# Decode attention beside a gated feed-forward block: all loads behind w_up's go through GpSimd's software queue

## The chip, the core and the metric

The kernel runs on one core of a Trainium2 chip. A core has TensorE (PE, matrix products), VectorE (DVE), ScalarE (ACT), GpSimd (POOL) and SyncE (SP), each with an instruction queue of its own, and 16 DMA engines that move data between the chip's memory (HBM) and the core's on-chip memory (SBUF). Engines wait for each other by semaphores. A transfer is issued by an instruction in the queue of SyncE, ScalarE or GpSimd; on the first two hardware makes the list of row transfers from the instruction, on GpSimd software does. The metric is the device time of one execution, in microseconds (us); the time of a kernel is the median of several runs.

## The reference

Four sequences (B = 4), one new token each (512 numbers). Attention has 32 heads of 128 numbers over a cache of 4096 keys and values per head, all in 32-bit floats:

```python
q = (x @ wq).reshape(B, 1, 32, 128).transpose(0, 2, 1, 3)
p = softmax(einsum("bhqd,bhkd->bhqk", q, k_cache) * 128 ** -0.5)
a = einsum("bhqk,bhkd->bhqd", p, v_cache).transpose(0, 2, 1, 3).reshape(B, 1, 4096) @ wo
b = (gelu(x @ w_gate) * (x @ w_up)) @ w_down
g = sigmoid((x * gate_w).sum(-1, keepdims=True))
out = g * a + (1 - g) * b
```

The inner size of the feed-forward block is 1792. The two caches are 268 MB each and are read once; the weights are some 28 MB together.

## The kernel before

**Tiles.** The attention is cut into NT = 32 tiles, each of one sequence and four heads. Tile i has one load of keys, K(i), and one of values, V(i), of 128 rows of 64 KiB each (8 MiB). K(i) lies 32 partitions per head and 128 keys per partition. For a tile DVE multiplies the keys by the query (`products`, L384), sums over the 128 numbers of each key (`sums`, L390), and finds the greatest score (`soft_max`, L395 to L397); ACT makes the exponentials (L402); PE multiplies them with the values (`pv`, L416). `products` and `sums` are each done in two parts, a quarter of 4096 numbers per partition (`shared` is True) and the rest of 12288.

**One buffer for everything.** All loads go into one SBUF tensor, `big`. The two places for keys overlap by a quarter, the part called shared: K(i+1) may be loaded as soon as the shared quarter of K(i) is summed. There is one place for values: V(i) may be loaded when `pv(i - 1)` is through. Before the tiles the same space holds wq, w_gate and w_up; behind them w_down and wo.

**The order.** `Plan` takes the steps in the order of the program text (`add`), and works out for each step which earlier steps it must wait for, by the ranges that they read and write. `loop` turns the repeated tiles on PE, DVE and ACT into loops; SyncE's and GpSimd's steps are written out one by one. An engine works through its own queue in order. Every load is made by `load` (L258), so all 76 of them stand in SyncE's queue in the order: wq, K(0), w_gate, w_up, K(1), V(0), K(2), V(1), ..., V(31), w_down, and wo in eight pieces. ACT issues the two small loads x and gate_w (L292, L293). GpSimd has six small instructions at the start and one at the end.

**The start.** wq lands, PE forms the queries (L330), DVE and PE spread them (L347 to L374). w_gate and w_up may be loaded when PE has read wq. K(1) waits for `sums(0, True)`. In between, with i = 0, stands the feed-forward block's first half:

```python
        products(i, False)
        if i == 0:
            gates()
            ffn_up(0)
            ffn_up(1)
            ffn_gelu()
            load_kv("v", 0)
        sums(i, False)
```

`ffn_up(0)` and `ffn_up(1)` are PE's products with w_gate and w_up (L518). `ffn_gelu` works in w_up's place (L530 to L537), so it begins when PE has read w_up. V(0) takes space that the block's intermediate numbers lie in, so it waits for its last step, the transposition into `hT` (L537). K(2) waits for `sums(1, True)`, which stands behind all that on DVE.

**The end.** `load_d` and `load_w` load w_down and wo; PE multiplies with them (L497, L505), and SyncE stores the result in two parts (L616).

Of the kernel before, what the change touches and what calls it, by code (L numbers as in the profile page):

```python
# [19 lines left out]
class Plan:  # L20
# [18 lines left out]
    def add(self, engine, emit, reads=(), writes=(), lane=None, unit=1):  # L39
        lane = lane or engine  # L40
        self.units[lane] = unit
        row = self.by_lane.setdefault(lane, [])
        step = Step(lane, engine, emit, self.turn if engine in self.loops else None)
        step.at = len(row)
        need = {}
        for accesses, writing in ((reads, False), (writes, True)):
            for name, lo, hi in accesses:
                for other, a, b, wrote in self.past.get(name, ()):
                    if a < hi and lo < b and (wrote or writing):
                        if other.lane == engine and engine == "pe":  # L50
                            continue
                        if other.lane == engine and not wrote:
                            continue
                        need[other.lane] = max(need.get(other.lane, -1), other.at)
        seen = self.seen[engine]
        for l, n in sorted(need.items(), key=lambda x: -len(self.by_lane[x[0]])):
            if seen.get(l, -1) >= n:
                continue
            other = self.by_lane[l][n]
            other.asked = True  # L60
            step.waits[l] = n
            seen[l] = n
            for k, v in self.knew[other].items():
                seen[k] = max(seen.get(k, -1), v)
        step.waits = {l: n for l, n in step.waits.items()
                      if not any(self.knew[self.by_lane[m][k]].get(l, -1) >= n for m, k in step.waits.items() if m != l)}
        self.knew[step] = dict(seen)
        self.knew[step][lane] = step.at
        if row and lane == engine:
            for k, v in self.knew[row[-1]].items():  # L70
                if k != lane:
                    self.knew[step][k] = max(self.knew[step].get(k, -1), v)
        for accesses, writing in ((reads, False), (writes, True)):
            for name, lo, hi in accesses:
                old = self.past.get(name, [])
                if writing:
                    old = [x for x in old if not (lo <= x[1] and x[2] <= hi)]
                self.past[name] = old + [(step, lo, hi, writing)]
        row.append(step)
        self.steps.append(step)  # L80
        return step
# [51 lines left out]
def tile_gated_mix(tc: tile.TileContext, x, kc, vc, wq, wo, w_gate, w_up, w_down, gate_w, out):  # L133
    nc = tc.nc
# [107 lines left out]
    plan = Plan(nc)  # L242
    add = plan.add
    V, A, T, G = nc.vector, nc.scalar, nc.tensor, nc.gpsimd
# [11 lines left out]
        return g if plan.k is None else plan.k  # L256

    def load(dst, src, writes, lane):  # L258
        return add("sp", lambda: nc.sync.dma_start(dst, src), (), writes, lane=lane, unit=16)

    def load_kv(kind, i):
        src = (vc, kc)[kind == "k"]
        a = KB_ * (i % 2) if kind == "k" else VA if i < NT - 1 else 0
        s = src[i % B, HT * (i // B):HT * (i // B) + HT].rearrange("h (p r) d -> (h p) (r d)", p=PH)
        load(place(a, TW), s, [z(a, TW)], "vl" if kind == "v" and i == NT - 1 else kind)
# [7 lines left out]
    def load_f(s):  # L273
        load(place((F0, F1)[s], KC * F), (w_gate, w_up)[s].rearrange("(p c) n -> p (c n)", c=KC),
             [z((F0, F1)[s], KC * F)], f"f{s}")

    def load_d():
        load(place(D0, FC * DM), w_down.rearrange("(p i) n -> p (i n)", i=FC), [z(D0, FC * DM)], "k")
# [326 lines left out]
    for h in range(2):  # L605
# [4 lines left out]
        for c, move in ((2 * h + 1, act), (2 * h, dve)):  # L610
            dst, read, write = res[:B, slice(*COLS[c])], [(("acc", "po0")[h], 0, C4)], [("res", *COLS[c])]
# [48 lines left out]
```

## Time and profile before

| | |
|---|---|
| median of 3 runs | 1308.88 us (1308.85 to 1308.92) |
| the profiled execution | 1308.95 us, its span 1307.5 us |
| DVE busy | 1158.2 us (89% of the span) |
| PE busy | 353.2 us (27%) |
| ACT busy | 87.3 us (7%) |
| POOL busy | 0.7 us, 6 instructions |
| moved by DMA | 564.83 MB, 432 GB/s over the span |

The profile names instructions by engine, line of the kernel and tiles (`big<-in_A_k_cache` is a load of keys). The span runs from the first to the last instruction; the execution's own time is 1.45 us longer. An idle time is given with what ended it. The DMA view of a stretch shows how busy the 16 engines were in 40 equal slices, and for each queue the packets (one row of a load, or the 4 bytes that raise a semaphore), their bytes and the share of the 16 engines' time that they took; a packet counts where it starts, so a short window can show over 100%. q1 is SyncE's queue and q10 is ACT's.

### The profile page before, as it was taken

How to read it: one execution, taken by the hardware profiler on the slowest of the kernel's cores; microseconds unless marked ns; L12 is line 12 of the kernel's file. 1: busy time of each engine (PE TensorE's matmuls, PEld its weight loads, DVE VectorE, ACT ScalarE, POOL GpSimd, SP SyncE). 2: the span in 40 equal slices, each digit the busy share in tenths (PEclk: the TensorE clock that was granted, in tenths of full speed). 3: DMA queues.
4: the chain of work that ended last, by engine and by line, in shares of the span. 5: the costliest groups of instructions: out<-in, count | busy, mean ns of one | idle time of the engine just before them, and what ended most of it. 6: DMA issues, size and time to landing. Idle time of an engine off the chain costs nothing.

```text
span 1307.5 us, 6158 instructions
## 1 busy us (share of the span) xinstructions
PE 353.2 (27%) x2512; PEld 100.2 (8%) x2512; DVE 1158.2 (89%) x303; ACT 87.3 (7%) x291; POOL 0.7 (0%) x6
## 2 busy tenths in 40 slices
PE   2303233212232211322321222321133232123227
PEld 0100001000010000100000000100001000000003
DVE  2799999999899998989989898998989899898992
ACT  0000000000000000000000000000000000000001
POOL 0000000000000000000000000000000000000000
PEclk9656666556666656666655666665666665666668
DMA  9999999999999999999999999999999999999998
GB/s 418 424 439 439 430 441 428 439 427 441 425 441 425 441 427 439 435 433 439 431 439 429 439 427 441 425 441 425 441 433 433 439 431 439 431 439 428 439 428 370
DMA packets 10986, 564.83 MB, mean 432 GB/s; under 512 B 1232, under 2 KB 1752, under 8 KB 1888
## 3 DMA queue, kind: packets, MB, share of 16 engines
q1 hardware_dynamic: 10960, 564.67, 99.8%
q8 instruction: 7, 0.11, 0.0%
q14 instruction: 3, 0.02, 0.0%
q10 hardware_dynamic: 16, 0.02, 0.0%
HBM read 564.67 MB, written 0.01 MB: 432 GB/s over the span
## 4 chain that ended last, share of the span: by engine, by line
DMA 72%; DVE 26%; PE 1%; issue 1%; ACT 0%; SPq 0%; DVEq 0%
DMA big<-in_A_k_cache 66%; DVE sc L390 13%; DVE big L384 12%; DMA big<-in_B_w_up 2%; DMA big<-in_A_wo 2%; DMA big<-in_A_wq 2%; PE po L330 1%; PE q L518 0%; PE acc L505 0%; PE wide L497 0%; PE po L505 0%; DVE hT L537 0%; DVE big L535 0%; DVE big L530 0%; DVE big L534 0%
## 5 line engine op out<-in xcount | busy, mean ns | idle before, releaser
L384 DVE TENSOR_TENSOR big<-big,qb 128x4096 f32<-128x4096 f32 x64 | 556.0, 8687 | 89.5 <-DMA big<-in_A_k_cache 89.5
L390 DVE TENSOR_REDUCE sc<-big 128x32 f32<-128x4096 f32 x64 | 555.9, 8686 | 2.3
L416 PE MATMUL po<-big,PM 128*32 128x512 f32 x2048 | 295.9, 743 | 899.9 <-DMA big<-in_A_v_cache 899.9
L416 PEld LDWEIGHTS po<-big,PM 128*32 128x32 f32 x2048 | 72.7, 133 | 1116.7 <-DMA big<-in_A_v_cache 823.9
L402 ACT ACTIVATE PM<-sc,nb 32x128 f32<-32x128 f32 x128 | 67.2, 525 | 476.4 <-DVE nb L397 430.7
L424 ACT ACTIVATE o<-po 128x512 f32<-128x512 f32 x16 | 9.6, 597 | 446.2 <-PE po L416 446.2
L402 ACT ACTIVATION_READ_ACCUMULATOR PM<-sc,nb 32x1 f32 x128 | 26.1, 204 | 0.0
L374 ACT ACTIVATE qb<-q 128x512 f32<-128x512 f32 x8 | 4.8, 597 | 245.7 <-PE q L372 245.7
L347 DVE TENSOR_TENSOR big<-po,amask 128x512 f32<-128x512 f32 x2 | 1.3, 686 | 18.0 <-PE po L330 18.0
L433 PE MATMUL sm<-o,sel 128*16 128x128 f32 x128 | 15.4, 273 | 5.8 <-ACT o L424 5.8
L518 PE MATMUL q<-big,xT 128*32 128x448 f32 x64 | 9.5, 751 | 18.0 <-DMA big<-in_B_w_gate 13.0
L330 PE MATMUL po<-big,xT 128*32 128x512 f32 x64 | 8.7, 702 | 18.9 <-DMA big<-in_A_wq 18.9
L433 PEld LDWEIGHTS sm<-o,sel 128*16 128x16 f32 x128 | 11.7, 97 | 14.4 <-ACT o L424 13.1
L615 DVE COPY res<-acc 4x144 f32<-4x144 f32 x1 | 0.3, 296 | 12.7 <-PE acc L505 12.7
L372 PE MATMUL q<-QM,hc 128*128 128x512 f32 x16 | 9.3, 666 | 4.2 <-DVE hc L368 4.2
L395 DVE TENSOR_REDUCE m<-sc 128x1 f32<-128x128 f32 x32 | 9.2, 286 | 1.1
L440 DVE RECIPROCAL ri<-sm 16x1 f32<-16x1 f32 x8 | 1.2, 156 | 8.7 <-PE sm L435 8.7
L396 DVE STREAM_TRANSPOSE mt<-m 128x32 f32<-128x32 f32 x32 | 6.8, 212 | 1.1
L397 DVE TENSOR_REDUCE nb<-mt 128x1 f32<-128x32 f32 x32 | 5.9, 186 | 1.1
L497 PE MATMUL wide<-big 128*32 128x512 f32 x46 | 5.6, 596 | 1.9 <-DMA big<-in_A_wo 1.9
L320 DVE TENSOR_TENSOR big<-big 4x512 f32<-4x512 f32 x1 | 0.7, 679 | 4.8 <-DMA big<-in_gate_w 4.8
L518 PEld LDWEIGHTS q<-big,xT 128*32 128x32 f32 x64 | 2.9, 146 | 23.8 <-issue 23.8
(74 smaller groups left out, 59.8 us busy)
## 6 DMA issues: line engine op xcount, KB each, us to landing
big<-in_A_wo SPq DMA_DIRECT2D x1, 4096.0 KB, 28.3
big<-in_B_w_gate SPq DMA_DIRECT2D x1, 3584.0 KB, 18.9
big<-in_B_w_up SPq DMA_DIRECT2D x1, 3584.0 KB, 28.1
big<-in_B_w_down SPq DMA_DIRECT2D x1, 3584.0 KB, 19.0
big<-in_A_wo SPq DMA_DIRECT2D x1, 1792.0 KB, 26.4
big<-in_A_wo SPq DMA_DIRECT2D x1, 1280.0 KB, 29.1
big<-in_A_k_cache SPq DMA_DIRECT2D x32, 29.7
big<-in_A_v_cache SPq DMA_DIRECT2D x32, 29.3
```

Of the source, the lines that this page charges most:

```text
L330: last = T.matmul(PO[s][32 * j:32 * j + 32].rearrange("p j d -> p (j d)"), xTf[:, c, :32], w[:, n0:n0 + HB * D], start=c == 0, stop=c == K ...
L372: pe(lambda: T.matmul(q.rearrange("p b d -> p (b d)"), HC.rearrange("p h k -> p (h k)"), QM.rearrange("p b d -> p (b d)"), start=True, sto ...
L384: dve(lambda: V.tensor_tensor(k, k, QB[:, b:b + 1, :].to_broadcast([P, r1 - r0, D]), op=OP.mult), m + t("qb"), m)
L390: dve(lambda: V.tensor_reduce(SC[i % 2][:, r0:r1], k, axis=AX.X, op=OP.add), [z(KA(i) + r0 * D, (r1 - r0) * D)], [(f"sc{i % 2}", r0, r1)])
L395: dve(lambda: V.tensor_reduce(M1[n], SC[n], axis=AX.X, op=OP.max), t(f"sc{n}"), t(f"m1{n}"))
L396: dve(lambda: V.transpose(MT, M1[n].to_broadcast([P, PH])), t(f"m1{n}"), t("mt"))
L397: dve(lambda: V.tensor_reduce(NB[n], MT, axis=AX.X, op=OP.max, negate=True), t("mt"), t(f"nb{n}"))
L402: last = A.activation(PM[:, PZ:].rearrange("p (c m) -> p c m", m=32)[s, :, h:RJ * HT:HT], SC[n][s, :].rearrange("p (c j) -> p c j", j=RJ), ...
L416: last = T.matmul(PO[n][32 * c:32 * c + 32].rearrange("p j d -> p (j d)"), PM[:, m0:m0 + 32], place(VAT(i) + j * N, N), start=b == 0 and j ...
L424: act(lambda: A.activation(O[n], PO[n], AF.Copy), t(f"po{n}"), t(f"o{n}"))
L433: T.matmul(sm[:B * HT, :D], selv[:, j, m0:m0 + B * HT], O[n][:, j, :], start=(n, j) == (0, 0), stop=(n, j) == (N - 1, RJ - 1))
L518: last = T.matmul(q.rearrange("p b d -> p (b d)")[32 * j:32 * j + 32, :FG], xTf[:, c, :32], place((F0, F1)[s] + c * F + j * FG, FG), start ...
```

## The change

`load` counts the steps that SyncE has. The first four loads (wq, K(0), w_gate, w_up) stay with it, all later ones are issued by GpSimd, whose transfers have a queue of their own; their semaphores get new names. Nothing else differs: the same 76 loads of the same shapes, into the same places, behind the same waits.

```diff
     def load(dst, src, writes, lane):
-        return add("sp", lambda: nc.sync.dma_start(dst, src), (), writes, lane=lane, unit=16)
+        e, queue = ("sp", nc.sync) if sum(x.engine == "sp" for x in plan.steps) < 4 else ("pool", G)
+        return add(e, lambda: queue.dma_start(dst, src), (), writes, lane=lane if e == "sp" else "p" + lane, unit=16)
```

One line more in the code makes every line number behind L259 greater by one. SyncE's queue at the start, before (a row names the line, the operation, the tile and its source, the shape, and the queues whose semaphores it waits for: `lane_dve` is DVE's progress, `lane_pe` PE's):

```order
L259 DMA big<-in_A_k_cache 128x16384
L627 UNCONDITIONAL_BRANCH
L259 DMA big<-in_B_w_gate 128x7168 [waits barrier_Pool_Activation_PE_DVE_SP_release,lane_pe]
L259 DMA big<-in_B_w_up 128x7168
L259 DMA big<-in_A_k_cache 128x16384 [waits lane_dve]
L259 DMA big<-in_A_v_cache 128x16384 [waits lane_dve]
L259 DMA big<-in_A_k_cache 128x16384 [waits lane_dve]
```

The rows are K(0), w_gate, w_up, K(1), V(0) and K(2): K(1) stands behind w_up in one queue. SyncE's queue from the same place, now:

```order
L260 DMA big<-in_A_k_cache 128x16384
L628 UNCONDITIONAL_BRANCH
L260 DMA big<-in_B_w_gate 128x7168 [waits barrier_Pool_Activation_PE_DVE_SP_release,lane_pe]
L260 DMA big<-in_B_w_up 128x7168
L617 DMA out<-res 4x288 [waits lane_fin0]
L617 DMA out<-res 4x224 [waits lane_fin1]
```

Behind w_up only the two stores are left. GpSimd's queue, before, from its own instructions for the identity matrix to its end:

```order
L298 MEMSET ident 128x128 [waits barrier_Pool_Activation_PE_DVE_SP_gather]
L299 ISA [waits lane_pool]
L299 AFFINE_SELECT ident<-ident 128x128
L635 ISA [waits issued]
L635 ISA
```

Between the identity matrix and the clearing of the semaphores at the end there was nothing. GpSimd's queue now, from the same place:

```order
L299 MEMSET ident 128x128 [waits barrier_Pool_Activation_PE_DVE_SP_gather]
L300 ISA [waits lane_pool]
L300 AFFINE_SELECT ident<-ident 128x128
L260 DMA big<-in_A_k_cache 128x16384 [waits lane_dve]
L260 DMA big<-in_A_v_cache 128x16384 [waits lane_dve]
L260 DMA big<-in_A_k_cache 128x16384 [waits lane_dve]
L260 DMA big<-in_A_v_cache 128x16384 [waits lane_pe]
```

K(1), V(0), K(2), V(1) and all later loads have come here, in their old order and with their old waits. K(1) and w_up now stand in two different queues, and no wait of K(1) holds it until w_up has landed.

## The prediction

> **What bounds the kernel now.** I read the page first, then the chain in order of time, then the timeline of one turn of the loop, then the DMA view in short windows. From the page: the span, the busy share of the 16 DMA engines in 40 slices, the one queue that carries nearly everything, and the shares of the chain.
>
> ```profile
> span 1307.5 us, 6158 instructions
> DMA  9999999999999999999999999999999999999998
> q1 hardware_dynamic: 10960, 564.67, 99.8%
> DMA 72%; DVE 26%; PE 1%; issue 1%; ACT 0%; SPq 0%; DVEq 0%
> ```
>
> The engines are never idle: SyncE's queue q1 moves 564.67 MB and its packets fill 99.8% of the span. So the end moves only if the stream gets a hole, or if its packets get slower. One turn of the loop in the chain (start, length, what):
>
> ```profile
> 624.78 4.43 DVE sc L390
> 629.23 29.75 DMA big<-in_A_k_cache
> 659.00 4.44 DVE big L384
> ```
>
> The turn after it in the timeline, with what ended an idle stretch in brackets:
>
> ```profile
> 667.80 12.95 DVE L384 TENSOR_TENSOR big<-big,qb 128x12288 f32<-128x12288 f32 x1
> 667.91 0.33 SPq L259 DMA_DIRECT2D big<-in_A_k_cache  x1
> 686.99 0.33 SPq L259 DMA_DIRECT2D big<-in_A_v_cache  x1
> 697.59 4.43 DVE L384 TENSOR_TENSOR big<-big,qb 128x4096 f32<-128x4096 f32 x1 [2.11 <-DMA big<-in_A_k_cache]
> ```
>
> A K load is issued 8.9 us after the K before it lands (659.00, 667.91) and takes 29.7 us, because a V load is ahead of it. The DMA view of 667 to 706 us gives the packets:
>
> ```profile
> DMA packets 291, 16.97 MB, mean 435 GB/s; under 512 B 32, under 2 KB 32, under 8 KB 32
> q1 hardware_dynamic: 291, 16.97, 100.4%
> ```
>
> Without the 32 semaphore packets these are 259 packets of 64 KiB. 39 us x 16 engines x 1.004 / 259 = 2.42 us each. Every load has 128 rows, 8 per engine, so a K or V load takes 8 x 2.42 = 19.36 us. The V ahead of the K of 667.91 therefore ends at 659.0 + 19.4 = 678.4: that K was issued 10.5 us early. V (686.99, needed by 697.7) is 10.7 us early.
>
> **The change part by part.**
>
> *Issuing in the loop.* What is added is the time from POOL's release to the first packet of its list; I call it L. For SyncE: the DMA view of 0 to 12 us (slices of 0.3 us) shows the first packets at 1.5 us, and SyncE issues wq at 0.74:
>
> ```profile
> DMA  0000099950000000990000009950000099900000
> ```
>
> ```profile
> 0.74 0.40 SPq L259 DMA_DIRECT2D big<-in_A_wq  x1
> 2.46 0.20 POOL L298 MEMSET ident<- 128x128 f32 x1 [2.02 <-POOLq L627]
> ```
>
> So L is some 0.9 us there, taken as the lower bound. For software, the trace shows no POOL issue. If the list of each of 16 engines cost one POOL operation of 0.20 us (the row above), L would be 0.9 + 3.2 = 4.1 us, the upper bound; I take 2.0, nearer the hardware, since the rows per engine are only eight. In the loop L costs nothing at any of these: 10.5 us of queue covers it. If L passed 10.5 us, each K would open a hole.
>
> *The end.* The stream's last loads go through POOL too.
>
> ```profile
> 1266.94 0.33 SPq L259 DMA_DIRECT2D big<-in_B_w_down  x1
> 1273.41 0.80 SPq L259 DMA_DIRECT2D big<-in_A_wo  x2
> 1277.62 9.31 PE L416 MATMUL po<-big,PM 128*32 128x512 f32 x64 [10.73 <-DMA big<-in_A_v_cache]
> ```
>
> ```profile
> big<-in_A_wo SPq DMA_DIRECT2D x1, 4096.0 KB, 28.3
> big<-in_B_w_down SPq DMA_DIRECT2D x1, 3584.0 KB, 19.0
> ```
>
> The last V lands at 1277.6, so w_down, issued at 1266.9, has 10.7 us. Behind it w_down and the first wo piece (7.5 MiB by the page's list of issues) keep the engines busy for 18 us more, to 1296 (435 GB/s in the row above). Seven further issues of 2 us, the first of them released at 1273.4 as now, are through by 1288. Nothing is added. SyncE's own order loses 72 issues of some 0.33 us, which waited for others and never were the late thing; no gain.
>
> *Two queues at the start.* Here the price lies. w_gate and w_up stay on SyncE, the second K (K1) goes to POOL, so K1 no longer stands behind w_up but beside it.
>
> ```profile
> 31.91 0.43 SPq L259 DMA_DIRECT2D big<-in_B_w_up  x1
> 50.88 12.95 DVE L384 TENSOR_TENSOR big<-big,qb 128x12288 f32<-128x12288 f32 x1
> 50.99 0.33 SPq L259 DMA_DIRECT2D big<-in_A_k_cache  x1
> 60.16 4.90 PE L518 MATMUL q<-big,xT 128*32 128x448 f32 x32 [4.99 <-DMA big<-in_B_w_up]
> 65.12 0.63 DVE L530 TENSOR_TENSOR big<-big 128x448 f32<-128x448 f32 x1 [0.31 <-PE q L518]
> 69.82 0.33 SPq L259 DMA_DIRECT2D big<-in_A_v_cache  x1
> 92.50 0.33 SPq L259 DMA_DIRECT2D big<-in_A_k_cache  x1
> ```
>
> Two rows of the DMA view, of 51.5 to 54.5 us (queue, packets, MB, share) and of 56.8 to 59.8 us (40 slices of 0.075 us):
>
> ```profile
> q1 hardware_dynamic: 48, 1.38, 106.2%
> ...
> GB/s 0 0 1147 382 1147 765 765 382 765 382 382 0 0 0 0 0 2622 874 0 4369 1748 874 1256 874 874 0 0 0 0 0 0 0 0 0 0 0 0 874 0 0
> ```
>
> K1 is issued at 50.99, w_up lands at 60.0 (31.91 + 28.11, PE starts at 60.16). The first window has 48 packets of w_up (3 x 16 x 1.062 / 48 = 1.06 us each); the second shows K1's first burst at 58.0. So w_up's eight packets run from 58.0 - 8 x 1.06 = 49.5 on.
>
> Do two queues share an engine? This trace shows it once: ACT issues gate_w while wq streams.
>
> ```profile
> 1.34 0.26 ACTq L293 DMA_DIRECT2D big<-in_gate_w  x1
> 10.61 0.68 DVE L320 TENSOR_TENSOR big<-big 4x512 f32<-4x512 f32 x1 [4.75 <-DMA big<-in_gate_w]
> ```
>
> The DMA view in three windows, of 7.1 to 8, 8 to 9.5 and 9.5 to 10.5 us (q1 is SyncE's queue, q10 ACT's):
>
> ```profile
> q1 hardware_dynamic: 16, 1.05, 268.8%
> q10 hardware_dynamic: 4, 0.01, 2.3%
> ...
> DMA packets 0, 0.00 MB, mean 0 GB/s; under 512 B 0, under 2 KB 0, under 8 KB 0
> ...
> q1 hardware_dynamic: 16, 1.05, 241.9%
> q10 hardware_dynamic: 4, 0.00, 0.2%
> ```
>
> gate_w's data goes out behind wq's second packet (bursts at 1.5, 4.8, 7.2 in the row of 0 to 12 us: one moving and one already taken), then a whole wq packet runs on each engine, then gate_w's semaphore goes, and DVE resumes at 10.61. The queues alternate packet by packet; a small load landed 9 us after its issue.
>
> Applied to w_up: K1's list is there at 51.0 + 2.0 = 53.0, when (53.0 - 49.5) / 1.06 = 3.3, so the fourth packet moves and the fifth is taken. Packets six to eight and the semaphore each wait for one K1 packet: 4 x 2.42 = 9.7 us. On engines a little behind it is five, 12.1, and the landing waits for the slowest engine. I take 4.5, so w_up lands D = 10.9 us later, at 70.9.
>
> Who waits: PE L518, then all of the gelu (L530 waits for PE already, by 0.31 us), so everything on DVE behind it moves by D: V0's issue from 69.82 to 80.7, K2's from 92.50 to 103.4. The total of w_up and K1 is unchanged, so the engines run dry at 58.0 + 19.4 = 77.4. V0's packets start at 80.7 + 2.0 = 82.7: a hole of 5.3 us. V0 ends at 102.1, K2 starts at 103.4 + 2.0 = 105.4: 3.3 us more. Before, K2 started at 77.4 + 19.4 = 96.8, 4.3 us after its issue. So the sum is D + L - 4.3 = 10.9 + 2.0 - 4.3 = 8.6 us. K3 then has DVE 10.9 late but the stream 8.6 late; its queue covers that, and DVE gains back its idle (2.11 in the row at 697.59, each turn). A hole in a full stream is never given back, so the end moves by 8.6.
>
> With L = 0.9, D is 5.5 packets: 13.3 + 0.9 - 4.3 = 9.9. With L = 4.1, 2.5 packets: 6.0 + 4.1 - 4.3 = 5.8. A slower list meets less of w_up, so the sum hardly depends on L; half a packet more or less gives 4.6 to 11.1. No step can win: the moved work waits for no issue.
>
> By the Trainium skill (DMA: Bandwidth & Descriptors, Specifications) the software path's first byte comes at about 1 us against 0.6; by that estimate L is 1.3 and the sum about 9 us. No row here shows it.
>
> **The rivals.**
>
> *Not slower.* The engines empty the list that came first before they turn to POOL's. Then D is 0, V0 needs 71.8 against 77.4 and K2 94.5 against 96.8: no hole until L passes 4.3. 1308.9 us. Against it: gate_w did get between wq's packets, with eight wq packets listed first. 0.13.
>
> *Whole loads alternate.* A K1 list goes out as one: D = 19.4, sum 19.4 + 2.0 - 4.3 = 17.1, 1326 us. For hardware lists the gate_w rows speak against it; POOL's list is unseen. 0.08. The Trainium skill (DMA: Bandwidth & Descriptors, Queues, rings and completion order) has an engine switch only after a packet of typically 9 to 17 descriptors, which would be this case; the trace switched after one 64 KiB row.
>
> *DVE holds POOL's list back.* K is released exactly when the 12.95 us product starts (667.80, 667.91). If POOL could not write during it, K would come 12.95 + 2.0 = 14.95 us after release, against 10.5: 4.5 us x 31 K loads = 140, 1449 us. It decides from a hold of 8.5 us on. No row shows POOL working beside DVE. 0.06. The Trainium skill (SBUF — State Buffer, Who interferes with whom) reports such a lock for copies and not for a product of two tensors.
>
> *Shorter pieces.* If software cuts rows, each piece pays an overhead. The DMA view of 1299.5 to 1300.5 us has 10 KiB packets:
>
> ```profile
> DMA packets 41, 0.42 MB, mean 420 GB/s; under 512 B 0, under 2 KB 0, under 8 KB 0
> q1 hardware_dynamic: 41, 0.42, 98.7%
> ```
>
> 16 x 0.987 / 41 = 0.385 us, against 0.378 at the 64 KiB rate: about 7 ns a piece. Pieces of 4 KiB would add 15 x 0.007 = 0.1 us to 2.42, or 4%: 63 loads x 19.36 x 0.04 = 50 us, 1359 us. 0.08.
>
> **How the numbers follow.** The profiled execution took 1308.95 us (span 1307.5), the median is 1308.88. 1308.9 + 8.6 = 1317.5 us, the alternation packet by packet, 0.62. The range takes in no change at the low end and whole loads at the high end: 1308.5 to 1328, leaving out the lock, the pieces and 0.03 for a gain that no row supports. 0.2% (2.6 us) is about what a measurement of this kernel can tell. Slower 0.62 + 0.08 + 0.06 + 0.08 = 0.84, same 0.13, faster 0.03.
>
> **What would show it.** Right: w_up landing near 71, V0 issued near 81, K2 near 103, two holes in the DMA row before 110 us, and a turn of the loop still 38.6 us with 2.42 us packets. Wrong: w_up landing at 60; or a loop turn that is longer; or the new queue's packets below 64 KiB.

## The result and the profile after

The changed kernel takes 1317.34 us (median of 4 runs, 1315.28 to 1318.02) against 1308.9 us: 1.0061 times as long, with a 95% interval of 1.0049 to 1.0073. That is 8.4 us more. The profiled execution took 1318.02 us, with a span of 1316.6. First the page of the changed kernel: the span, the busy share of the DMA engines in 40 slices, the two queues, the shares of the chain, and GpSimd's group of K issues (count, busy us, mean ns, idle time before and its releaser).

```profile
span 1316.6 us, 6158 instructions
DMA  9988999999999999999999999999999999999998
q0 software_dynamic: 9984, 540.55, 94.9%
q1 hardware_dynamic: 592, 24.13, 4.3%
DMA 71%; DVE 26%; PE 2%; issue 1%; ACT 0%; SPq 0%; DVEq 0%
L260 POOL DMA_DIRECT2D big<-in_A_k_cache x31 | 16.5, 532 | 613.2 <-DVE sc L391 613.2
```

Two eights in the third and fourth slice (66 to 132 us) are all that has changed in the busy row: behind them the stream is as full as before. GpSimd spends 0.53 us on an issue. The start, in the timeline of the changed kernel:

```profile
51.48 0.67 POOL L260 DMA_DIRECT2D big<-in_A_k_cache  x1 [48.28 <-DVE sc L391]
69.84 6.04 PE L519 MATMUL q<-big,xT 128*32 128x448 f32 x32 [13.72 <-DMA big<-in_B_w_up]
75.94 0.63 DVE L531 TENSOR_TENSOR big<-big 128x448 f32<-128x448 f32 x1 [10.94 <-PE q L519]
79.68 0.94 DVE L538 STREAM_TRANSPOSE hT<-big 128x448 f32<-128x448 f32 x1
80.93 0.53 POOL L260 DMA_DIRECT2D big<-in_A_v_cache  x1 [28.78 <-DVE hT L538]
103.59 0.53 POOL L260 DMA_DIRECT2D big<-in_A_k_cache  x1 [22.13 <-DVE sc L391]
```

PE begins with w_up at 69.84, where it began at 60.16. The gelu follows at 75.94 (65.12 before), V0 is issued at 80.93 (69.82), K2 at 103.59 (92.50). DVE stood idle for 10.94 us, where it had been 0.31. What happened to w_up is in the DMA view of the changed kernel, in the windows 55.2 to 57.8, 57.8 to 59, 59 to 61.2, 61.2 to 62.3, 62.3 to 64.8, 64.8 to 66.4 and 66.4 to 70 us (q0 is GpSimd's queue and carries K1, q1 is SyncE's and carries w_up):

```profile
q0 software_dynamic: 16, 1.05, 94.2%
q1 hardware_dynamic: 3, 0.09, 7.7%
...
q1 hardware_dynamic: 13, 0.37, 71.9%
...
q0 software_dynamic: 16, 1.05, 109.9%
q1 hardware_dynamic: 3, 0.09, 9.1%
...
q1 hardware_dynamic: 12, 0.34, 72.4%
...
q0 software_dynamic: 16, 1.05, 96.7%
q1 hardware_dynamic: 4, 0.03, 2.7%
...
q0 software_dynamic: 15, 0.98, 141.7%
q1 hardware_dynamic: 13, 0.06, 8.7%
...
q0 software_dynamic: 17, 1.11, 71.4%
q1 hardware_dynamic: 2, 0.00, 0.0%
```

A round of 16 K1 packets, one on each engine, then a round of w_up's rows, twice over. Behind the third K1 round come w_up's semaphores, with its last two rows among them: 3 of the 4 packets of q1 between 62.3 and 64.8 us and 11 of the 13 between 64.8 and 66.4 us are semaphores, and the last two come as late as 68 to 70. Those two hold w_up back for all. The two holes are in the DMA view of 76 to 110 us, slices of 0.85 us:

```profile
DMA  1000000970890990950900900905900009910950
```

A slice counts the packets that start in it, so the ends come from shorter windows. K1's last round starts near 75.0 us and V0's first packets at 82.1: with 2.42 us a packet the first hole runs from some 77.4 to 82.1 us. V0's last round starts at 99.7 to 100.2 us and K2's first packets at 104.8, so the second runs from some 102.4 to 104.8. (Single zeros between are slices in which no packet starts.) Much later a turn of the loop reads as before, only later:

```profile
667.83 4.42 DVE L385 TENSOR_TENSOR big<-big,qb 128x4096 f32<-128x4096 f32 x1 [3.16 <-DMA big<-in_A_k_cache]
676.63 12.95 DVE L385 TENSOR_TENSOR big<-big,qb 128x12288 f32<-128x12288 f32 x1
677.01 0.53 POOL L260 DMA_DIRECT2D big<-in_A_k_cache  x1 [18.64 <-DVE sc L391]
```

Before, this K landed at 659.00: the lag is 8.83 us here and 9.1 us at the span's end. Almost nothing is added over the second half of the kernel.

### The profile page after: what moved, and what is told of

It reads as the page before. It is cut to its first block, busy times and chain, and to the rows that moved or that the text cites. A ratio compares the mean times of both kernels' runs of the same rounds, so it can differ in the third digit from the quotient of the medians.

```text
span 1316.6 us, 6158 instructions
## 1 busy us (share of the span) xinstructions
PE 354.3 (27%) x2512; PEld 100.4 (8%) x2512; DVE 1158.4 (88%) x303; ACT 87.3 (7%) x291; POOL 38.8 (3%) x78
## 3 DMA queue, kind: packets, MB, share of 16 engines
q0 software_dynamic: 9984, 540.55, 94.9%
## 4 chain that ended last, share of the span: by engine, by line
DMA 71%; DVE 26%; PE 2%; issue 1%; ACT 0%; SPq 0%; DVEq 0%
DMA big<-in_A_k_cache 65%; DVE sc L391 13%; DVE big L385 12%; DMA big<-in_B_w_up 3%; DMA big<-in_A_wo 2%; DMA big<-in_A_wq 2%; PE po L331 1%; PE q L519 0%; PE acc L506 0%; PE wide L498 0%; PE po L506 0%; DVE hT L538 0%; DVE big L536 0%; DVE big L531 0%; DVE big L535 0%
## 5 line engine op out<-in xcount | busy, mean ns | idle before, releaser
L260 POOL DMA_DIRECT2D big<-in_A_v_cache x32 | 16.9, 528 | 607.6 <-PE po L417 560.4
L260 POOL DMA_DIRECT2D big<-in_A_k_cache x31 | 16.5, 532 | 613.2 <-DVE sc L391 613.2
L531 DVE TENSOR_TENSOR big<-big 128x448 f32<-128x448 f32 x1 | 0.6, 626 | 10.9 <-PE q L519 10.9
```

Source lines behind the costliest of these rows:

```text
L260: return add(e, lambda: queue.dma_start(dst, src), (), writes, lane=lane if e == "sp" else "p" + lane, unit=16)
```

## The experiments

Theory A is the prediction's: the price is paid once, at the start, because two queues share the engines packet by packet, w_up is the loser, and DVE hangs on w_up. Theory B: software issue costs something with each load. Theory C: it is the software queue that alternates. Theory D: the second queue takes a share of bytes or goes first. The diffs are against the changed kernel, that of the third experiment against the kernel before, and `...` stands for lines left out. In the first four, `load` counts its calls in `n`. The line numbers of the timelines differ with each edit.

**K1 back to SyncE, the other 71 loads with GpSimd.** So that K1 can have a semaphore of its own, the first turn of the loop is written out, here and in the second and fifth experiment.

```diff
-        e, queue = ("sp", nc.sync) if sum(x.engine == "sp" for x in plan.steps) < 4 else ("pool", G)
+        n = plan.loads = getattr(plan, "loads", 0) + 1
+        e, queue = ("sp", nc.sync) if n <= 5 else ("pool", G)
...
-        return g if plan.k is None else plan.k
+        return g if plan.k is None else plan.k + 1
...
-        plan.turn = (i - 1) // B if 0 < i < NT - B + 1 else None
+        plan.turn = (i - 1) // B - 1 if B < i < NT - B + 1 else None
```

> The second key load K1 goes back to SyncE behind w_up; V0 and all later loads stay with GpSimd. (The first turn of the loop is written out instead of looped, so that K1 can have a semaphore of its own.) Theory A (the whole price is that K1 in a second queue alternates with w_up and so delays DVE): w_up lands near 60 us again, no hole before 110 us, 1309 to 1310 us. V0 now alternates with the tail of K1 instead, by about two packets (4.8 us), which lands K1 near 84 us, just when DVE wants it (83.6). Theory B (the software queue is dearer for every load, or slower): 71 of the 72 moved loads are still with GpSimd, so 1317 us.

Measured: 1310.1 us, 1.0009 times before (interval 1.0000 to 1.0019). Its timeline:

```profile
59.05 4.84 PE L520 MATMUL q<-big,xT 128*32 128x448 f32 x32 [2.82 <-DMA big<-in_B_w_up]
69.69 0.67 POOL L261 DMA_DIRECT2D big<-in_A_v_cache  x1 [66.49 <-DVE hT L539]
84.32 4.43 DVE L386 TENSOR_TENSOR big<-big,qb 128x4096 f32<-128x4096 f32 x1 [1.19 <-DMA big<-in_A_k_cache]
```

w_up is on time again, V0 now meets the tail of K1 instead, and K1 lands at 84.3, as worked out beforehand. With 71 of 72 loads still in software the loss has shrunk from 8.4 to about 1 us: theory B falls as an account of the loss.

**K1 alone with GpSimd**, all else with SyncE (first turn written out as above).

```diff
...
+        e, queue = ("pool", G) if n == 5 else ("sp", nc.sync)
...
```

> K1 alone goes through GpSimd, every other load through SyncE (first turn written out as above). Theory A: w_up lands near 70 us as in the changed kernel, DVE is some 11 us late, V0 and K2 open two holes; with SyncE's 0.9 us from issue to first packet in place of GpSimd's 1.5 the sum is 0.6 us less than in the changed kernel, 1316 to 1317 us. Theory B: one load of 72 is left with GpSimd, 1309 us.

Measured: 1316.33 us, ratio 1.0052 (1.0035 to 1.0069). One load of 72 makes nearly all of the loss. Its timeline:

```profile
69.93 4.92 PE L520 MATMUL q<-big,xT 128*32 128x448 f32 x32 [13.23 <-DMA big<-in_B_w_up]
79.61 0.33 SPq L261 DMA_DIRECT2D big<-in_A_v_cache  x1
102.16 0.33 SPq L261 DMA_DIRECT2D big<-in_A_k_cache  x1
```

**K1 with ScalarE**, whose queue is filled by hardware, all else with SyncE.

```diff
...
+        e, queue = ("act", nc.scalar) if n == 5 else ("sp", nc.sync)
...
```

> As before the change, but K1 is issued by ScalarE, whose queue is a hardware queue too. Theory A (any second queue does it): K1's list is there 0.6 us earlier than GpSimd's, so it meets as much of w_up or one packet more; w_up lands at 70 to 72 us and the time is 1316 to 1319 us. Theory C (alternation is a property of the software queue): w_up lands at 60 us, 1309 us.

Measured: 1316.39 us, ratio 1.0062 (1.0045 to 1.0078). No load of this kernel goes through software, and the loss is the same as with K1 alone on GpSimd. Theory C falls: a second hardware queue does it too. w_up lands near 68.6 us, earlier than the 70 to 72 that were expected, and PE's pass over it is longer (6.08 us). Its timeline:

```profile
50.98 0.36 ACTq L261 DMA_DIRECT2D big<-in_A_k_cache  x1
68.72 6.08 PE L520 MATMUL q<-big,xT 128*32 128x448 f32 x32 [13.22 <-DMA big<-in_B_w_up]
102.24 0.33 SPq L261 DMA_DIRECT2D big<-in_A_k_cache  x1
```

**w_gate and w_up with GpSimd too**, so that K1 stands behind w_up in one queue; only wq and K0 stay with SyncE.

```diff
...
+        e, queue = ("sp", nc.sync) if n <= 2 else ("pool", G)
...
```

> w_gate and w_up go through GpSimd as well, so that K1 stands behind w_up in one queue again; SyncE keeps wq and K0. Theory A: K1 no longer meets w_up, but w_gate (listed near 33 us) meets the second half of K0, whose last packets wait for three or four of w_gate's 1.06 us packets; K0 lands 3 to 4 us late, near 45.5, and all of DVE with it. K2 needs DVE late by under 4.3 less 0.6 us to open no hole, so the price is 0 to 1.5 us: 1309 to 1310.5 us. Theory B: all but two loads are with GpSimd, 1317 us or more.

Measured: 1310.17 us, ratio 1.0008 (0.9999 to 1.0018). K0 is now the one that meets a second queue; it lands at 45.32 (45.5 was expected), and K2's issue moves by 3.1 us only:

```profile
45.32 4.43 DVE L386 TENSOR_TENSOR big<-big,qb 128x4096 f32<-128x4096 f32 x1 [8.73 <-DMA big<-in_A_k_cache]
60.29 5.82 PE L520 MATMUL q<-big,xT 128*32 128x448 f32 x32 [4.13 <-DMA big<-in_B_w_up]
95.60 0.53 POOL L261 DMA_DIRECT2D big<-in_A_k_cache  x1 [22.15 <-DVE sc L392]
```

**K1 in four pieces**, with the changed kernel's queues (first turn written out).

```diff
-        load(place(a, TW), s, [z(a, TW)], "vl" if kind == "v" and i == NT - 1 else kind)
+        m = TW // 4 if (kind, i) == ("k", 1) else TW
+        for c in range(0, TW, m):
+            load(place(a + c, m), s[:, c:c + m], [z(a + c, m)],
+                 f"k1{c}" if m < TW else "vl" if kind == "v" and i == NT - 1 else kind)
...
```

> The changed kernel, with K1 loaded in four pieces of 16 KiB rows (first turn written out). Theory A (one packet of the one queue for one of the other): each of w_up's last three or four packets now waits for a K1 packet of 0.61 us instead of 2.42, so w_up is 2 to 2.5 us late, DVE about as much, and 2.5 + 1.5 - 4.3 is below nothing: no hole, 1309 to 1310 us. Rival D (GpSimd's queue goes first, or takes its share whatever the packets' size): w_up again near 70 us, 1317 us.

Measured: 1309.75 us, ratio 1.0005 (0.9996 to 1.0015). Same two queues, same bytes, and nearly all of the loss is gone: the price is the length of the other queue's packet. Its timeline, with w_up 2.6 us late:

```profile
51.22 2.24 POOL L260 DMA_DIRECT2D big<-in_A_k_cache  x4 [48.02 <-DVE sc L394]
62.76 4.81 PE L522 MATMUL q<-big,xT 128*32 128x448 f32 x32 [6.42 <-DMA big<-in_B_w_up]
95.14 0.53 POOL L260 DMA_DIRECT2D big<-in_A_k_cache  x1 [22.01 <-DVE sc L394]
```

**w_up in two halves**, of 14 KiB rows, otherwise the changed kernel (SyncE keeps five loads instead of four, since w_up is two).

```diff
-        e, queue = ("sp", nc.sync) if sum(x.engine == "sp" for x in plan.steps) < 4 else ("pool", G)
+        e, queue = ("sp", nc.sync) if sum(x.engine == "sp" for x in plan.steps) < 5 else ("pool", G)
...
+        src, m = (w_gate, w_up)[s].rearrange("(p c) n -> p (c n)", c=KC), KC * F // (1 + s)
+        for c in range(0, KC * F, m):
+            load(place((F0, F1)[s] + c, m), src[:, c:c + m], [z((F0, F1)[s] + c, m)], f"f{s}")
```

> The changed kernel, with w_up loaded in two halves of 14 KiB rows, so that twice as many of its packets are left when K1's list arrives (all on SyncE). Theory A: w_up's end waits for five to eight K1 packets instead of three or four, D is 13 to 19 us, and the time is D + 1.1 + 1.5 - 4.3 + 0.6 more than before: 1321 to 1327 us. Rival D (share of bytes): the same bytes are left, so w_up lands as in the changed kernel, 1317 us.

Measured: 1323.48 us, ratio 1.0119 (1.0102 to 1.0136). The same bytes in twice the packets lose 14.6 us instead of 8.4; theory D falls on this side as well. Its timeline:

```profile
31.87 0.91 SPq L260 DMA_DIRECT2D big<-in_B_w_up  x2
76.11 5.37 PE L520 MATMUL q<-big,xT 128*32 128x448 f32 x32 [19.29 <-DMA big<-in_B_w_up]
109.20 0.53 POOL L260 DMA_DIRECT2D big<-in_A_k_cache  x1 [22.13 <-DVE sc L392]
```

**GpSimd late in the loop.** Eight fills of a spare tile stand between the release and the issue of K(8) to K(31); in a second kernel, sixteen.

```diff
...
+        if kind == "k" and i >= 8:
+            for _ in range(8):
+                add("pool", lambda: G.memset(scratch, 0.0), (), [z(a, TW)] + t("scratch"))
```

> The changed kernel, with eight fills of a spare tile (1024 numbers per partition) on GpSimd between DVE's release and the issue of K(8) to K(31). With d for the delay that they make, the hole per K load should be d + 1.5 - 10.4 where that is above nothing. At 0.9 us a fill (an estimate from the 0.20 us of 128 numbers) d is 7 to 8 us: no hole, 1317 us, as the changed kernel. Rival B (each load's issue time is paid in the loop): 24 x 7.5 = 180 us more.

> As the run before with sixteen fills: d is 14 to 16 us, past the 8.9 us that the queue covers, so each of 24 K loads opens a hole of 5 to 7 us: 1317 + 120 to 170 = 1437 to 1487 us. If the end does not move here, the cover is not the queue of the load ahead.

Measured: 1362.85 us with eight fills (ratio 1.0404, 1.0386 to 1.0422) and 1529.48 us with sixteen (1.1691, 1.1671 to 1.1710). Over the changed kernel's 1317.34 that is 45.5 / 24 = 1.9 us and 212.1 / 24 = 8.8 us per K load. Both were misses: with eight fills no hole was expected, and with sixteen 5 to 7 us per K load. The timelines, of eight fills and then of sixteen:

```profile
691.69 12.95 DVE L389 TENSOR_TENSOR big<-big,qb 128x12288 f32<-128x12288 f32 x1
691.83 8.01 POOL L269 MEMSET scratch<- 128x1024 f32 x8 [19.98 <-DVE sc L395]
700.14 0.53 POOL L261 DMA_DIRECT2D big<-in_A_k_cache  x1 [0.30 <-POOL scratch L269]
724.27 4.43 DVE L389 TENSOR_TENSOR big<-big,qb 128x4096 f32<-128x4096 f32 x1 [4.91 <-DMA big<-in_A_k_cache]
```

```profile
697.31 4.43 DVE L389 TENSOR_TENSOR big<-big,qb 128x4096 f32<-128x4096 f32 x1 [11.98 <-DMA big<-in_A_k_cache]
706.25 16.08 POOL L269 MEMSET scratch<- 128x1024 f32 x16 [27.21 <-DVE sc L395]
722.63 0.53 POOL L261 DMA_DIRECT2D big<-in_A_k_cache  x1 [0.30 <-POOL scratch L269]
745.03 4.43 DVE L389 TENSOR_TENSOR big<-big,qb 128x4096 f32<-128x4096 f32 x1 [12.20 <-DMA big<-in_A_k_cache]
```

With sixteen fills the engines are empty at the issue, and K still takes 745.03 - 722.63 = 22.4 us to land. From its landing to DVE's next product, which starts as the release comes, it is 8.8 us (697.31 to 706.11). A turn of 38.64 us therefore has 38.64 - 8.8 - 22.4 = 7.4 us in which a late issue is free, not the 8.9 of the expectation. The expectation left out what follows the last packet: K's first packets are at 723.8 (DMA view of 713 to 725 us), its eight per engine end near 743.7 (2.93 us for the first, 2.42 for the others), and K lands 1.3 us behind that. Sixteen fills make 16.5 us (706.11 to 722.63), 9.1 past the 7.4 and near the 8.8 found. Eight make 8.45 us (691.69 to 700.14), 1.0 past it. The rest of the 1.9 is in the landing: in the chain of that kernel the 24 delayed K loads take 23.3 us on average (21.9 to 25.1), 0.9 more than 22.4. Why they do is not shown.

## Why the prediction was right

The forecast was 1317.5 us and the mechanism is the one that it put first. Point by point:

- **w_up's lag D.** Predicted 10.9 us; measured 9.7 (PE waits until 69.84 instead of 60.16, and the chain has w_up landing at 69.7 instead of 60.0). The alternation packet by packet is shown by the windows above, and its size by the kernels with K1's packets made shorter and w_up's made more. Where 4.5 K1 packets were taken, the last two engines waited for four: 4 x 2.42 = 9.7.
- **How many packets of w_up stood behind.** Three, and the semaphore, was the count; it was two and the semaphore on most engines. Between 55.2 and 66.4 us q1 moves only 3 + 13 + 3 + 12 + 1 + 2 = 34 data packets, so six of eight had gone on each engine before K1's first. K1's list was there at about 51.1 + 1.5 = 52.6 (an estimate, with L as V0 has it below), but the engines went on with w_up until 55.6. The step "one moving and one already taken" was too small: about 3 us of packets went first. What made D come out near all the same is that two engines were one packet behind the others and the landing waits for the last.
- **From release to first packet, L.** Predicted 2.0; measured 1.5: V0 is released at 80.62 (79.68 + 0.94) and its first packets are at 82.1, in the DMA view of 80 to 84 us:

```profile
DMA  0000000000000000000009999990909090000000
q0 software_dynamic: 16, 1.05, 73.3%
```

- **The sum.** D + L - 4.3 was 8.6; with the measured terms it is 9.7 + 1.5 - 4.3 = 6.9. Two terms were missing, and they make up for D and L: PE's pass over w_up took 6.04 us where it took 4.90 (1.1 us), and the first packets after a hole are slow (4 x 16 x 0.733 / 16 = 2.93 us in the last row against 2.42: 0.5). 6.9 + 1.1 + 0.5 = 8.5; the lag of the profiled execution is 9.1, the median's 8.4. So the forecast's closeness is in part two errors that cancel; its place, its two holes and its size to within 2 us are not. The same terms give the other three losses: 9.8 + 0.0 + 0.9 - 4.3 + 0.6 = 7.0 for K1 alone with GpSimd (measured 7.3), 8.6 + 1.2 + 0.9 - 4.3 + 0.6 = 7.0 for K1 with ScalarE (7.3), and 15.9 + 0.5 + 1.5 - 4.3 + 0.5 = 14.1 for w_up in halves (14.5). In the first two V0 and K2 go through SyncE, with 0.9 us from issue to first packet (79.61 to 80.55 in the kernel with K1 alone) and first packets of 3.0 us.
- **PE's pass.** Its length does not follow the loss: it took 4.92 us in one kernel with the loss and 6.08 in another, and 5.82 in the one with the weights on GpSimd, which has none. It goes with the granted TensorE clock, which over the pass was 0.65 before and 0.53 in the changed kernel: 4.94 x 0.65 = 3.2 and 6.06 x 0.53 = 3.2, and in the two kernels with the loss 4.92 x 0.65 and 6.08 x 0.52 are 3.2 as well. Why the clock differs from run to run is open. Before, the 4.3 us between K2's issue and its first packet would have hidden such a difference; in the changed kernel K2 starts as soon as it is released and listed, and nothing does.
- **V0, K2 and the holes.** V0 was forecast at 80.7 and is at 80.9, K2 at 103.4 and is at 103.6. Holes of 5.3 and 3.3 us were forecast; they are about 4.7 and 2.4, each followed by slow first packets.
- **The loop.** No cost was forecast and none is there: the K of 677.01 is issued 9.2 us after the landing of the one before (8.9 before the change), the load ahead covers it, and the lag stays at 8.8 to 9.1. The cover was over-stated, though: 10.5 us of queue less the 1.5 of L is 9.0, and only 7.4 can be used.
- **The end.** No cost was forecast, and next to none is there: the last K lands 8.96 us later than before (1247.54 against 1238.58), where the middle had 8.83, and the span ends 9.1 later.

Of the rivals, "not slower" failed because the engines did not empty the older list first. "Whole loads" would have had all of w_up's rest behind K1; the Trainium skill (DMA: Bandwidth & Descriptors, Queues, rings and completion order) speaks of packets of typically 9 to 17 descriptors between two switches, and here both kinds of queue gave way after one row of 64 KiB. "DVE holds POOL's list back" is answered by K2, in the timeline and in the DMA view of 103.5 to 106.5 us:

```profile
103.21 12.95 DVE L385 TENSOR_TENSOR big<-big,qb 128x12288 f32<-128x12288 f32 x1
DMA  0000000000000000099990009990900000900000
```

K2 is released at 103.3, as DVE's product begins, and its first packets are at 104.8, 1.5 us later, while the product still runs for 11 us. V0, with no product of that kind beside it, took the same 1.5. The Trainium skill (SBUF — State Buffer, Who interferes with whom) says of a product of two tensors that it did not stall such a DMA; these rows agree. "Shorter pieces" is answered by the packets: in the row of 80 to 84 us 16 of them carry 1.05 MB, 64 KiB each. The pages' lines on all packets, before and now, show the one difference:

```profile
DMA packets 10986, 564.83 MB, mean 432 GB/s; under 512 B 1232, under 2 KB 1752, under 8 KB 1888
DMA packets 10602, 564.83 MB, mean 429 GB/s; under 512 B 1232, under 2 KB 1240, under 8 KB 1504
```

512 packets under 2 KB are gone and 128 of 2 to 8 KB have come. The only rows of such a size are the 4 x 128 of the four smallest pieces of wo (896 and 1152 bytes), so GpSimd's queue put four of these rows into one packet. The 9984 packets of q0 are then 68 loads of 128 rows and 16 semaphores and 4 loads of 32 packets and 16 semaphores: no row was cut.

What stays open: the changed kernel's runs spread over 2.7 us, those of before over 0.3 (PE's pass could make 1.1 of it, which no run shows); and the three experiments without the loss are still 0.8 to 1.1 us above before, with intervals that touch no change. Some small cost of software issue is therefore not excluded.

## What to carry to other kernels

A second DMA queue is no second pair of hands: while both have work, each engine takes one packet from each in turn, so a small load that is nearly done waits for as many of the other load's rows as it has packets left. Before moving a load to another queue, look for the load that it used to stand behind and ask what hangs on that one; if something does, keep both in one queue, or make the intruder's rows short. In a kernel whose DMA engines are never idle, a hole at the start is paid in full, while issue time in the middle is free as long as the load queued ahead lasts, here some 7 us a turn.

## What the runs showed of the hardware

- A second queue's first packet under load came some 3 us later than its list: K1 on GpSimd's queue was listed at about 52.6 us (an estimate) and moved from 55.6, while V0, with the engines idle, moved 1.5 us after its release.
- The first packets after an empty stretch took longer than the 2.42 us of the stream: 2.93 us on average in software's queue after a hole, 3.03 in hardware's at the start (the 16 packets of wq in the DMA view of 0.7 to 2.7 us take 151.3% of it).
- A load through software issue moves at the same pace as through hardware: 38.6 us for 16 MiB in both loops. The Trainium skill (DMA: Bandwidth & Descriptors, Specifications) puts the first byte at about 1 us against 0.6; from release to first packet these traces have 1.5 us against 0.9, a difference of 0.6.
- GpSimd's issue of a 128-row load took 0.53 us, of its first one 0.67.
- GpSimd's queue moved rows of 16, 28 and 64 KiB as one packet each, and four rows of 896 or 1152 bytes as one packet; in SyncE's queue each of those rows was a packet of its own.
